# Two samples of the input stored and loaded in blocks of 32 channels: a Fourier filter with a token router, on one core

## The chip, the core and the metric

The kernel runs on one core of a Trainium2 chip. The metric is the device time of one execution in microseconds (us). A run of this kernel varies by about 0.2% around its median, so a difference of less than 0.5% is hard to tell from no change.

## The reference

```python
X = np.fft.rfft(x, axis=1)                  # x: 8 samples, 3136 tokens, 256 channels, float32
Y = X * (filt_r + 1j * filt_i)[None]        # one filter value per frequency and channel
x = np.fft.irfft(Y, n=3136, axis=1)
scores = einsum('bsd,d->bs', x, w_gate)
for b in range(8):
    top = the 128 tokens of sample b with the highest scores
    ye = relu(x[b, top] @ w1) @ w2          # 256 -> 1024 -> 256
    out[b, top] += sigmoid(scores[b, top])[:, None] * ye
```

## The kernel before

**The transform.** 3136 tokens are 98 times 32. The transform of a sample is done in two levels. The *outer* level is a transform of length 98, done for a block of 32 channels at a time, so a sample has 8 blocks ("chunks", c = 0 to 7). The *inner* level is a transform of length 32 with the twiddle factors in its matrices, done for two frequency rows at a time (`i`, 13 of them, taken in pairs: i0 = 0, 2, ... 12; the text writes "step i0"). The work of a stage t is the inner level of sample t and, beside it, the outer level backwards of sample t-1 and forwards of sample t+1.

**A forward chunk** (`outer`) reads its 32 channels from the tile `X`, which holds one sample (4 MB): half 0 holds channels 0 to 127 (chunks 0 to 3), half 1 the others (chunks 4 to 7). Each chunk needs the sum and the difference of two parts of X ("folds", L449). The table `FOLD` says for each sample and chunk, by two letters for sum and difference, who makes them: `p` is GpSimd (POOL), `x` leaves the fold to TensorE, which then multiplies both parts and adds in PSUM, at two more matmuls for the pair. Then come the matmuls (`amm`, L475; 4 of them for `pp`, 6 with one `x`, 8 for `xx`) into a PSUM buffer (`pa`, `pz` or `pv`; there is one buffer of each; `ARING` says which), and a transpose by VectorE (DVE) from there into the tile `UU` (`tout`, L479). A fold into a tile of its own takes one of 3 buffers `s`.

**An inner step** is matmuls into `pz` (`zmm`, L378), two copies to `q` by ScalarE (ACT, L396), two products by DVE with the table `fa` (`pmul`, L400), two by POOL with the table `fb` (`qmul`, L403), matmuls into `pv` (`vmm`, L387), two copies from there by ACT (`vout`, L412) and four score sums by DVE (`gate`, L418). `pz` and `pv` have one buffer each: the next `zmm` waits until DVE has read `pz`, the next `vmm` until the four score sums have read `pv`.

**A backward chunk** is a DVE transpose (L440), matmuls and copies into `X`, from where a half is stored (L595) and the next sample's half is loaded (L600). The table `BACK` says by which form: for `e` one copy is made by ACT and a sum and a difference by DVE (L520); for `p` ACT makes two copies and POOL the sum and the difference (L536). The first ends with DVE as the last reader of the PSUM buffer, the second with ACT.

**The router and the two-layer network.** A search by thresholds (`select`) finds the 128 best tokens of a sample. `SELM` says for each sample whether its comparisons run on DVE (1) or ACT (0). The network on the chosen tokens runs at the end, after the last inner step.

**Order.** `op(...)` only appends a closure to a list; the time and cost arguments in it do nothing at run time. The table `ORDER`, a list of closure numbers, sets the order of the program on every engine. All direct transfers are issued by SyncE (SP), in that order. They share 8 completion semaphores in turn: transfer n+8 is issued only after transfer n has landed, and SP does nothing else while it waits.

**Start.** TensorE first runs 60 small matmuls on zeros (`WARM`, L1064), and later `FILL` groups of them between other work. SP issues half 1 of sample 0, the outer-level matrix (`wa`, 96 KB), half 0, then tables: `fa` and `fb` for steps 4 and 6 (1 MB each), `tf`, `wg`, `ti`, `fb` and `fa` for step 0 (512 KB each). Then comes sample 1 by halves, between the remaining tables. `raw` is a transfer of 8 KB that DVE casts (L1055) between two inner steps.

```python
X = const.tile([128, 2, N2, D // 2], F32, name="X")
def load(when, b, h, bias=0.0):
    def f():
        if b < B:
            nc.sync.dma_start(out=X[:, h].rearrange("p n d -> p (n d)"), in_=x[b, :, h, :N2 * HD])
    op(when, "sp", 5.2, f, ["boot"], [("x", h, c) for c in range(h * n, h * n + n)], lat=2, bias=bias)
```

## Time and profile before

| | |
|---|---|
| median of 3 runs | 465.06 us (464.37 to 466.39) |
| profiled execution | 467.14 us |
| its span in the trace | 465.4 us, so 1.74 us lie around it |
| TensorE busy / DVE / POOL / ACT | 438.7 / 373.4 / 296.7 / 258.2 us |
| granted TensorE clock, mean | 0.997 of full speed |
| moved by DMA | 77.43 MB, 166 GB/s over the span |

A busy TensorE is not one at its peak: small matmuls on zeros count as busy, and matmuls overlap. Idle time of an engine costs something only where others wait for it, so the chain of waits and the timeline of a stretch say more than the shares.

### The profile page before, as it was taken

What the parts mean: (1) busy time and instruction counts of PE and PEld (TensorE: products, weight loads), DVE (VectorE), ACT (ScalarE), POOL (GpSimd) and SP (SyncE); (2) the same over time, 40 slices, a digit from 0 to 9 for tenths busy, and PEclk for the clock granted to TensorE, in tenths of its full rate; (3) what the DMA queues carried; (4) which work ended last, traced back from release to release, by engine and by line L of the source; (5) the groups of instructions that cost most, each with busy time, mean ns of one, the idle gap of its engine ahead of it and who ended that gap; (6) DMA issues with size and microseconds to landing.
All of it is one profiled execution on the core that took longest, in us unless ns stands there. A gap on an engine that the chain in (4) does not pass through costs nothing.

```text
span 465.4 us, 10712 instructions
## 1 busy us (share of the span) xinstructions
PE 438.7 (94%) x4066; PEld 233.8 (50%) x4066; DVE 373.4 (80%) x1079; ACT 258.2 (55%) x611; POOL 296.7 (64%) x262
## 2 busy tenths in 40 slices
...
GB/s 339 372 417 423 208 180 40 2 183 149 265 94 287 32 165 193 140 182 161 208 101 220 135 224 83 238 119 239 87 53 7 156 155 192 176 37 148 164 24 56
DMA packets 61063, 77.43 MB, mean 166 GB/s; under 512 B 3284, under 2 KB 56788, under 8 KB 58324
## 3 DMA queue, kind: packets, MB, share of 16 engines
...
q0 software_dynamic: 768, 2.10, 1.5%
...
HBM read 49.80 MB, written 26.94 MB: 165 GB/s over the span
## 4 chain that ended last, share of the span: by engine, by line
PE 53%; DVE 17%; POOL 9%; issue 6%; DMA 6%; ACT 3%; POOLq 0%; DVEq 0%; SPq 0%; ACTq 0%
PE pv L387 13%; PE py L573 10%; PE pa L475 9%; PE pz L378 7%; DVE rj L418 6%; DMA X<-in_x_dram 4%; DVE t L440 4%; POOL q L403 3%; DVE UU L479 3%; POOL s L449 3%; POOL X L449 2%; DVE y L400 2%; PE pv L953 2%; PE pa L983 2%; DMA out_dram<-X 2%
## 5 line engine op out<-in xcount | busy, mean ns | idle before, releaser
L403 POOL TENSOR_TENSOR q<-q,fb_sb 128x512 f32<-128x512 f32 (+1 forms) x104 | 130.9, 1276 | 67.5 <-ACT q L396 60.9
L449 POOL TENSOR_TENSOR s<-X 113x512 f32<-113x512 f32 x60 | 76.0, 1273 | 55.8 <-DMA X<-in_x_dram 51.2
L573 PE MATMUL py<-t,c_sb 128*98 128x512 f32 x186 | 100.8, 624 | 3.2 <-ACT X L576 2.4
L418 DVE SCALAR_TENSOR_TENSOR rj<-pv,wg_sb 128x256 bf16<-128x256 f32 x199 | 83.6, 420 | 13.9 <-ACT UU L412 7.3
L479 DVE STREAM_TRANSPOSE UU<-pa 128x1024 f32<-128x1024 f32 x59 | 73.3, 1243 | 23.8 <-PE pa L475 23.5
L396 ACT COPY q<-pz 128x512 f32<-128x512 f32 (+1 forms) x104 | 56.3, 586 | 51.5 <-PE pz L378 49.6
L412 ACT COPY UU<-pv 128x512 f32<-128x512 f32 x96 | 51.7, 589 | 56.2 <-PE pv L387 56.0
L440 DVE STREAM_TRANSPOSE t<-UU 128x1024 f32<-128x1024 f32 x64 | 78.8, 1232 | 3.1 <-PE py L573 1.2
L475 PE MATMUL pa<-X,c_sb 49*64 49x512 f32 x344 | 79.8, 601 | 0.4 <-DVE rj L418 0.3
L400 DVE TENSOR_TENSOR y<-pz,fa_sb 128x512 f32<-128x512 f32 (+1 forms) x104 | 67.9, 674 | 8.5 <-ACT q L396 8.5
L387 PE MATMUL pv<-y,ti_sb 64*64 64x256 f32 x796 | 68.7, 386 | 4.2 <-DVE rj L418 3.1
L576 ACT COPY X<-py 98x512 f32<-98x512 f32 x93 | 54.2, 583 | 28.2 <-PE py L573 13.3
L387 PE MATMUL pv<-q,ti_sb 64*64 64x256 f32 x796 | 66.6, 377 | 2.8 <-POOL q L403 2.8
L378 PE MATMUL pz<-UU,tf_sb 64*64 64x256 f32 x800 | 60.9, 395 | 5.4 <-DVE y L400 2.8
L475 PE MATMUL pa<-s,c_sb 49*64 49x512 f32 x220 | 59.1, 606 | 1.3 <-DVE UU L479 1.2
L449 POOL TENSOR_TENSOR X<-X 113x512 f32<-113x512 f32 x42 | 53.2, 1271 | 1.6
L378 PEld LDWEIGHTS pz<-UU,tf_sb 64*64 64x64 f32 x800 | 29.0, 131 | 39.8 <-issue 11.7
L387 PEld LDWEIGHTS pv<-y,ti_sb 64*64 64x64 f32 x796 | 29.9, 132 | 33.5 <-issue 9.5
L573 PEld LDWEIGHTS py<-t,c_sb 128*98 128x98 f32 x186 | 23.9, 163 | 38.0 <-issue 11.5
L387 PEld LDWEIGHTS pv<-q,ti_sb 64*64 64x64 f32 x796 | 34.6, 133 | 15.1 <-POOL q L403 4.2
L679 ACT ACTIVATE junk<-R,nb 128x392 bf16<-128x392 f32 x48 | 30.0, 625 | 12.0 <-DVE nb L698 11.1
L475 PEld LDWEIGHTS pa<-X,c_sb 49*64 49x64 f32 x344 | 20.1, 132 | 15.3 <-issue 10.6
...
## 6 DMA issues: line engine op xcount, KB each, us to landing
...
```

Source lines behind the costliest of these rows:

```text
L378: nc.tensor.matmul(half(z, k)[o, hi], lhsT=tf_sb[p, l], rhs=urow(b, l, 0, D)[p], start=True, stop=True)
L387: nc.tensor.matmul(half(v, k)[o, j], lhsT=ti_at[p, t, i, hi], rhs=y[p, hi], start=t == 0, stop=t == 1)
L396: nc.scalar.copy(out=q[:np_], in_=half(h["z"], k)[:np_])
L400: nc.vector.tensor_tensor(out=y[:np_], in0=half(h["z"], k)[:np_], in1=fa_sb[:np_, i], op=ALU.mult)
L403: nc.gpsimd.tensor_tensor(out=h["q", k][:np_], in0=h["q", k][:np_], in1=fb_sb[:np_, i], op=ALU.mult)
L418: nc.vector.scalar_tensor_tensor(out=rj, in0=half(h["v"], k)[:, j], scalar=1.0, in1=wg_sb, op0=ALU.mult, op1=ALU.mult, accum_out=urow(b, l ...
L440: nc.vector.transpose(out=h["t"].rearrange("p d (l j) -> p d l j", j=2), in_=uchan(b_out, c))
L449: (nc.gpsimd if fold[k] == "p" else nc.vector).tensor_tensor(out=out, in0=two[0], in1=two[1], op=(ALU.add, ALU.subtract)[k])
L475: nc.tensor.matmul(a[o, w].rearrange("p (n d) -> p n d", d=CW), lhsT=lhs[p], rhs=rhs[p], start=n == 0, stop=n == len(terms) - 1)
L479: nc.vector.transpose(out=uchan(b_in, c), in_=h["a"].rearrange("p w (n d) -> p d n w", d=CW))
L573: nc.tensor.matmul(yp[:N1], lhsT=cc["wi"][:, :N1], rhs=h["t"][:, n * CY:(n + 1) * CY].rearrange("p a b -> p (a b)"), start=True, stop=True)
L576: nc.scalar.copy(out=X[:N1, hx, :, at], in_=e["y"][:N1])
```

## The change

1. In DRAM (`kernel`, on the host) and in SBUF (`Xc`), samples 0 and 1 lie by chunk: the 32 channels of a chunk are 4 KB in one row per partition. Samples 2 to 7 lie by halves as before.
2. Each of these two samples comes in 8 transfers of 512 KB, one per chunk, in place of 2 of 2 MB. Folds and matmuls of the two samples read the chunk's own piece.
3. A new ORDER, and with it other letters in `FOLD`, `BACK`, `SELM`, the tables of PSUM buffers (`BRING`, `YRING`, `VRING`, `ARING`) and 8 groups of filling matmuls (47) in place of 12 (57).

```diff
-        "pp pp xp xx pp xp xp xp",
-        "xp px xx pp xp xx pp pp",
-        "xp pp px pp xp xx pp px",
-        "pp pp pp pp px px xp xp",
+        "pp pp xx xx pp xp xp xp",
+        "xp px xp xx pp xx pp pp",
+        "xp pp pp pp xp xx pp pp",
+        "pp pp pp pp px pp xp xp",
...
-    BACK=["ffffffff", "ffffffff", "ffffffff", "ffffffff", "ffffffff", "ffffffff", "peqegggg", "ppppffff"],
+    BACK=["ffffffff", "ffffffff", "ffffffff", "ffffffff", "ffffffff", "ffffffff", "ppqegggg", "ppppffff"],
...
-    SELM=[0, 1, 1, 0, 0, 1, 1, 1],
+    SELM=[0, 0, 1, 0, 0, 1, 1, 1],
...
-    FILL=[6, 8, 12, 5, 5, 2, 2, 2, 3, 4, 2, 6],
+    FILL=[7, 12, 5, 5, 2, 3, 7, 6],
...
+    Xc = X.rearrange("p t n d -> p (t n d)").rearrange("p (c h n d) -> p c h n d", c=D // CW, h=2, d=CW)
...
-            two = Xh[:RW2, hx, 0, :, at], Xh[:RW2, hx, 1, :, at]
+            xin = [Xc[:, c, k] if b_in < 2 else Xh[:, hx, k, :, at] for k in range(2)]
+            two = [xin[k][:RW2] if b_out < 0 else Xh[:RW2, hx, k, :, at] for k in range(2)]
...
+        def piece(c):
+            nc.sync.dma_start(out=Xc[:, c].rearrange("p h n d -> p (h n d)"), in_=x[b, :, h, c % n * N2 * CW:(c % n + 1) * N2 * CW])
+
         n = HD // CW
+        if b < 2:
+            for c in range(h * n, h * n + n):
+                op(when + .01 * (c % n), "sp", 5.2 / n, lambda c=c: piece(c), ["boot"], [("x", h, c)], lat=2, bias=bias)
+            return
...
-    data["x"][..., :-XPAD] = xs.reshape(B, 128, N2, 2, D // 2).transpose(0, 1, 3, 2, 4).reshape(B, 128, 2, -1)
+    for b in range(B):
+        n = 2 if b >= 2 else 8
+        data["x"][b, ..., :-XPAD] = xs[b].reshape(128, N2, n, D // n).transpose(0, 2, 1, 3).reshape(128, 2, -1)
```

**The transfers at the start, on SP.** Before, from the first transfer to the first half of sample 1 (rows of 4096 floats are halves, 2048 and 1024 in `fa` and `fb` are 1 MB and 512 KB):

```order
L600 DMA X<-in_x_dram 128x4096
L1076 DMA c_sb<-in_cst_dram 128x192
L600 DMA X<-in_x_dram 128x4096
L1043 DMA fa_sb<-in_fri_dram 128x2048
L1043 DMA fb_sb<-in_fri_dram 128x2048
L1079 DMA tf_sb<-in_tf_dram 128x1600
L1080 DMA wg_sb<-in_moe_w_gate_dram 128x256
L1102 DMA ti_sb<-in_ti_dram 128x3328
L1043 DMA fb_sb<-in_fri_dram 128x1024 [waits DMAHW0_49]
L1043 DMA fa_sb<-in_fri_dram 128x1024 [waits DMAHW1_49]
L600 DMA X<-in_x_dram 128x4096 [waits DMAHW2_49,PE_49,Pool_49]
```

Now, to the same place (the pieces of sample 0 are those of chunks 5, 4, 6, then 0, 3, 2, 7, then 1; the first of sample 1 is chunk 1's):

```order
L605 DMA X<-in_x_dram 128x1024 x3
L1086 DMA c_sb<-in_cst_dram 128x192
L605 DMA X<-in_x_dram 128x1024 x4
L605 DMA X<-in_x_dram 128x1024 [waits DMAHW0_49]
L1053 DMA fa_sb<-in_fri_dram 128x2048 [waits DMAHW1_49]
L1053 DMA fb_sb<-in_fri_dram 128x2048 [waits DMAHW2_49]
L1089 DMA tf_sb<-in_tf_dram 128x1600 [waits DMAHW3_49]
L1112 DMA ti_sb<-in_ti_dram 128x3328 [waits DMAHW4_49]
L1090 DMA wg_sb<-in_moe_w_gate_dram 128x256 [waits DMAHW5_49]
L605 DMA X<-in_x_dram 128x1024 [waits DMAHW0_49,DMAHW6_49,PE_49,Pool_49]
L1053 DMA fa_sb<-in_fri_dram 128x1024 [waits DMAHW7_49]
L1053 DMA fb_sb<-in_fri_dram 128x1024
```

The tables for step 0 (the two rows of 1024 in `fa` and `fb`) moved from ahead of sample 1 to behind its first piece, and that piece waits for TensorE and POOL to be done with chunk 1 of sample 0. Behind these rows the other pieces of sample 1 come in the order 0, 3, 2, 4, 5, 6, 7, with `raw` and the two tables for step 2 between those of chunks 3 and 2, and the two tables of 1.25 MB for steps 8 to 12 between 4 and 5.

**POOL, from the end of the start into the first inner steps.** Before, from chunk 7's fold of sample 0 on:

```order
L449 TENSOR_TENSOR s<-X 113x512 [waits DMAHW2_49,PE_49]
L449 TENSOR_TENSOR X<-X 113x16x32 [waits Pool_49]
L449 TENSOR_TENSOR s<-X 113x512 [waits PE_49] x2
L449 TENSOR_TENSOR X<-X 113x16x32 [waits Pool_49]
L403 TENSOR_TENSOR q<-q,fb_sb 128x512 [waits DMAHW4_49,Activation_49]
L403 TENSOR_TENSOR q<-q,fb_sb 128x512 [waits Activation_49]
L403 TENSOR_TENSOR q<-q,fb_sb 128x512 [waits DMAHW0_49,Activation_49]
L403 TENSOR_TENSOR q<-q,fb_sb 128x512
L449 TENSOR_TENSOR s<-X 113x512 [waits DMAHW2_49,PE_49,Pool_49]
L403 TENSOR_TENSOR q<-q,fb_sb 128x512 [waits DMAHW5_49,PE_49,Activation_49]
```

Now, from chunk 7's fold on:

```order
L451 TENSOR_TENSOR s<-X 113x512 [waits DMAHW7_49,PE_49]
L451 TENSOR_TENSOR s<-X 113x512 [waits DMAHW4_49,PE_49]
L451 TENSOR_TENSOR X<-X 113x512 [waits Pool_49]
L451 TENSOR_TENSOR s<-X 113x512 [waits DMAHW0_49,PE_49]
L451 TENSOR_TENSOR X<-X 113x512 [waits Pool_49]
L404 TENSOR_TENSOR q<-q,fb_sb 128x512 [waits DMAHW2_49,Activation_49]
L404 TENSOR_TENSOR q<-q,fb_sb 128x512 [waits Activation_49]
L404 TENSOR_TENSOR q<-q,fb_sb 128x512 [waits DMAHW0_49,Activation_49]
L451 TENSOR_TENSOR s<-X 113x512 [waits DMAHW6_49,PE_49,Pool_49]
L404 TENSOR_TENSOR q<-q,fb_sb 128x512 [waits Activation_49]
L451 TENSOR_TENSOR s<-X 113x512 [waits DMAHW1_49,PE_49]
L404 TENSOR_TENSOR q<-q,fb_sb 128x512 [waits DMAHW4_49,PE_49,Activation_49]
```

One fold of sample 0 is gone (chunk 2's), and the first fold of sample 1 (chunk 1's) moved from behind the two products of step 0 to between them; the next two folds, of chunks 0 and 2, stand one product apart.

**DVE, in the backward chunks 1 and 3 of sample 6.** Before, from a backward transpose to the next four score sums (the two rows of L520 are the sum and the difference of chunk 1; those of chunk 3 follow behind the score sums):

```order
L440 STREAM_TRANSPOSE t<-UU 128x1024
L696 TENSOR_SCALAR ok,J<-pm 128x15
L698 TENSOR_SCALAR nb<-J,nd 128x1
L520 TENSOR_TENSOR X<-pa,X 113x16x32
L400 TENSOR_TENSOR y<-pz,fa_sb 128x512
L520 TENSOR_TENSOR X<-pa,X 113x16x32
L400 TENSOR_TENSOR y<-pz,fa_sb 128x512
L418 SCALAR_TENSOR_TENSOR rj,UU<-pv,wg_sb 128x256 x4
```

Now:

```order
L441 STREAM_TRANSPOSE t<-UU 128x1024
L401 TENSOR_TENSOR y<-pz,fa_sb 128x512
L706 TENSOR_SCALAR ok,J<-pm 128x15
L708 TENSOR_SCALAR nb<-J,nd 128x1
L401 TENSOR_TENSOR y<-pz,fa_sb 128x512
L419 SCALAR_TENSOR_TENSOR rj,UU<-pv,wg_sb 128x256 x4
```

Chunk 1's two operations have left DVE; the score sums come two operations earlier.

## Rows read from the trace of the kernel before

**Rows 1.** The page: TensorE's busy time; GB/s moved in 40 equal slices (11.635 us each).
```profile
PE 438.7 (94%) x4066; PEld 233.8 (50%) x4066; DVE 373.4 (80%) x1079; ACT 258.2 (55%) x611; POOL 296.7 (64%) x262
...
GB/s 339 372 417 423 208 180 40 2 183 149 265 94 287 32 165 193 140 182 161 208 101 220 135 224 83 238 119 239 87 53 7 156 155 192 176 37 148 164 24 56
```
**Rows 2.** Stretches: busy time of each engine (instructions), granted clock, DMA share, GB/s.
```profile
0.00:25.00 25.00, 22.95 (x240) 15.32 (x244) 9.46 (x8) 1.49 (x2) 12.84 (x16) 1.00 0.91 360
25.00:67.00 42.00, 38.35 (x498) 23.85 (x494) 29.57 (x73) 14.20 (x27) 32.43 (x26) 1.00 0.74 297
67.00:112.00 45.00, 45.00 (x412) 20.08 (x407) 40.07 (x94) 30.53 (x80) 25.04 (x20) 1.00 0.34 118
...
337.00:382.00 45.00, 38.83 (x406) 18.72 (x404) 42.56 (x139) 27.90 (x62) 23.07 (x19) 1.00 0.39 96
```
**Rows 3.** Timeline 0 to 25 us: start, duration, engine, line, [idle before, what ended it].
```profile
8.37 0.33 SPq L1043 DMA_DIRECT2D fb_sb<-in_fri_dram  x1
8.43 3.70 POOL L449 TENSOR_TENSOR s<-X 113x512 f32<-113x512 f32 x3 [7.50 <-DMA X<-in_x_dram]
...
9.92 0.65 PE L475 MATMUL pa<-X,c_sb 49*64 49x512 f32 x2
...
16.18 1.27 POOL L449 TENSOR_TENSOR X<-X 113x512 f32<-113x512 f32 x1
...
18.85 1.25 DVE L479 STREAM_TRANSPOSE UU<-pa 128x1024 f32<-128x1024 f32 x1 [1.82 <-PE pa L475]
...
19.98 1.28 POOL L449 TENSOR_TENSOR X<-X 113x512 f32<-113x512 f32 x1
...
24.73 1.14 PE L378 MATMUL pz<-UU,tf_sb 64*64 64x256 f32 x16 [0.55 <-DVE UU L479]
```
**Rows 4.** DMA packets started in 0 to 6 us, and in 26 to 28 us.
```profile
DMA packets 96, 1.57 MB, mean 262 GB/s; under 512 B 0, under 2 KB 0, under 8 KB 0
...
DMA packets 200, 0.88 MB, mean 441 GB/s; under 512 B 29, under 2 KB 29, under 8 KB 185
```
**Rows 5.** Timeline 30 to 61 us: TensorE's second matmuls of a step, POOL's folds of sample 1.
```profile
30.82 2.52 POOL L403 TENSOR_TENSOR q<-q,fb_sb 128x512 f32<-128x512 f32 x2 [1.73 <-ACT q L396]
...
34.49 0.66 PE L387 MATMUL pv<-y,ti_sb 64*64 64x256 f32 x8 [0.41 <-DVE rj L418]
...
35.04 1.26 POOL L449 TENSOR_TENSOR s<-X 113x512 f32<-113x512 f32 x1 [1.70 <-DMA X<-in_x_dram]
...
41.48 0.66 PE L387 MATMUL pv<-y,ti_sb 64*64 64x256 f32 x8
...
48.33 0.66 PE L387 MATMUL pv<-y,ti_sb 64*64 64x256 f32 x8 [0.26 <-DVE rj L418]
...
48.84 1.27 POOL L449 TENSOR_TENSOR s<-X 113x512 f32<-113x512 f32 x1 [0.24 <-DMA X<-in_x_dram]
...
60.29 0.66 PE L387 MATMUL pv<-y,ti_sb 64*64 64x256 f32 x8 [0.26 <-DVE rj L418]
```
**Rows 6.** Groups by form: POOL on rows in one piece (q) and on blocks of 32 (folds).
```profile
L403 POOL TENSOR_TENSOR q<-q,fb_sb 128x512 f32<-128x512 f32 x96 | 120.7, 1276 | 59.5 <-ACT q L396 52.9 <-PE pa L475 4.4 <-ACT UU L412 1.3
...
L449 POOL TENSOR_TENSOR s<-X 113x512 f32<-113x512 f32 x60 | 76.0, 1273 | 55.8 <-DMA X<-in_x_dram 51.2 <-PE pa L475 4.3
```
**Rows 7.** Timeline 354 to 366 us: the backward chunks 1 and 3 of sample 6.
```profile
354.49 2.52 POOL L403 TENSOR_TENSOR q<-q,fb_sb 128x512 f32<-128x512 f32 x2 [9.67 <-ACT q L396]
...
361.15 0.69 DVE L520 TENSOR_TENSOR X<-pa,X 113x512 f32<-113x512 f32 x1
...
362.35 0.68 DVE L520 TENSOR_TENSOR X<-pa,X 113x512 f32<-113x512 f32 x1
...
363.18 1.13 PE L505 MATMUL pa<-t,c_sb 64*64 64x512 f32 x8 [1.37 <-DVE X L520]
...
365.52 0.66 PE L387 MATMUL pv<-y,ti_sb 64*64 64x256 f32 x8 [0.30 <-DVE rj L418]
```
**Rows 8.** Waits, longest in total first: who waited for whom, us, times, longest.
```profile
POOL s L449 <- DMA X<-in_x_dram: 51.2, 11, 8.8
```

24 lines of the change are left out of this document (12 added, 12 removed), and 192 rows, old and new, of tables (FOLD, ORDER).

## The prediction

> **What bounds the kernel now.** I read the page first. TensorE is busy for 438.7 of 465.4 us [rows 1], so there is little idle time to win, and the question is where it lies. The stretches answer that [rows 2]: in 67 to 112 us TensorE is busy all the time. It idles for 2.0 us in the first 25 us, 3.7 us in 25 to 67 (zeros count as busy there, so the true wait is larger), and 6.2 us in 337 to 382. The granted clock is full in all of them. The change acts on the first two stretches and, by new letters, on the last.
>
> The start: the timeline [rows 3] shows POOL idle for 7.50 us until the first half of x has landed; SP saw it land at 8.37. TensorE comes to its first real matmul at 9.92, behind its 60 matmuls on zeros. POOL then makes ten folds from 8.43 to 21.26 (19.98 and 1.28), almost without a gap. Chunk 0's difference ends at 17.45 (16.18 and 1.27), and 1.40 us later, at 18.85, DVE begins the first of five transposes that follow each other without a gap; it had waited 1.82 us for TensorE. The first inner step starts behind them, at 24.73. So the start is a chain: landing, POOL's folds, DVE's transposes.
>
> The first inner steps: the matmuls into `pv` start at 34.49 (step 0), 41.48 (step 2), 48.33 and, two steps on, 60.29 [rows 5], mostly released by DVE's score sums: a loop through one PSUM buffer. POOL waited 1.70 us for the first half of sample 1, until 35.04, and 0.24 us for the second, until 48.84. From 11.6 to 46.5 us the transfers ran at 372 to 423 GB/s [rows 1], so all these bytes stand in one full queue, and their place in it says when they land.
>
> **The change, step by step.** *First landing.* By 6.0 us 1.57 MB had moved [rows 4]. That is three pieces of 0.524 MB. The first half (2.10 MB) would be moved by 7.3 at the 0.417 MB per us of the third slice [rows 1] and was seen at 8.37: a landing lag of 1.1 us. The third piece, chunk 6's, which POOL folds first, then lands at 7.1, and POOL starts 1.3 us earlier. Chunk 7's piece (3.77 MB with the matrix) lands at about 12.4, when POOL has done four folds (12.2).
>
> *POOL and DVE.* One fold of 1.27 us is gone (nine, not ten); chunk 2 costs TensorE two matmuls more, which lie beside the folds. Chunk 0's difference is POOL's seventh fold in both orders: 7.1 + 7 x 1.27 + 0.2 = 16.2 instead of 17.45. With 1.40 us to DVE and the same five transposes, the first inner step starts at 24.73 - 1.2 = 23.5. DVE now takes chunk 4 before chunk 6, which idles it for a microsecond ahead of 17.6, but not after. The smaller fold count therefore wins nothing beyond the earlier landing: chunk 1's folds end near 18.7, before TensorE wants them. Chunks in one piece don't make a fold faster: products on rows in one piece take 1276 ns, folds on blocks of 32 take 1273 [rows 6]. TensorE can't start earlier either; its zeros still end at 9.9.
>
> *Tables and sample 1.* By the slices 3.94, 8.27 and 13.1 MB have moved at 11.6, 23.3 and 34.9 us [rows 1]. In the old order the first half of sample 1 ends at 12.19 MB, which is 23.3 + 3.92 / 0.417 = 32.7 us, and the fold began at 35.04 after a wait for it: a lag of 2.3 us here. In the new order `fb` for step 0 ends at 10.61 MB (it stood at 9.57): moved by 28.9, landed by 30.0 with the lag of the start and by 31.2 with the later one. POOL wants it at 30.82 - 1.2 = 29.6. So it is 0.4 to 1.6 us late. Between the two products now stands chunk 1's fold, whose piece (9.57 MB) has landed by 28.7. Three operations of 1.27 us end at 33.8 or 35.0, and the matmuls of step 0 start then, not at 34.49 - 1.2 = 33.3. The new place of the fold pays back one operation later: chunk 1's DVE transpose (1.25 us) stood between steps 0 and 2 and now runs while DVE would wait for those matmuls. The interval of 6.99 us (34.49 to 41.48) falls to 5.7, and step 2 starts at 39.5 or 40.8: 2.0 or 0.7 us earlier than before. Chunk 2's fold, which stands in front of step 2's second product, needs a piece at 13.24 MB (35.2, landed 37.5), is done with the product at 40.0, and holds nothing up. I take the middle, **1.3 us**, because the lag was measured at both values. It contains the 1.2 us of the start.
>
> *Does it stay?* Behind step 2 the order on DVE is the old one, so the loop keeps its intervals. The pieces of chunks 5, 6 and 7 end at 16.9, 17.4 and 18.3 MB, so the last is moved at 47.1 and landed at 49.4, as late as the second half before (48.84). But that half held four chunks, and now only chunk 7 waits for the end; 11 us lie between that landing and the step at 60.29. The queue itself ends no sooner: no byte is saved, and the 14 additional issues stand on an SP that waits most of the time. From 67 us on TensorE is full [rows 2], so what is won before 67 stays won.
>
> *Sample 6, backward chunk 1.* TensorE waited 1.37 us at 363.18 for DVE's sum and difference (0.69 and 0.68 us), and the next matmuls into `pv`, at 365.52, again waited for DVE [rows 7]. With `p` those two operations move to POOL, which idled 9.67 us at 354.49, and one copy more to ACT. The gain lies between 0 (another wait takes the place) and 1.4; I take **0.9**, as both waits named DVE.
>
> *The rest.* Nine folds of sample 1 stay nine. One fold in all samples goes from TensorE to POOL, eight comparisons of sample 1's search from DVE to ACT, and 10 filling matmuls go: 0, since they lie beside a full TensorE or in idle time. The reordering of samples 2 to 7 swaps neighbours; its price isn't in any row. The bounds are a gain of the 6.2 us that TensorE idles in 337 to 382 and a loss of 8.8 us, POOL's longest wait for a half of x [rows 8]. I take 0, nearest to the stretch 67 to 112 where no idle time is left to move, and keep 1.5 us to either side for it.
>
> Sum: 1.3 + 0.9 = 2.2 us, or 467.14 - 2.2 = 464.9 for an execution like the profiled one. That one lay 2.1 us above the median of the runs, 465.06, which gives **462.9**.
>
> **A rule that speaks against it.** Transfers of 4 KB rows ran beside each other without loss: in 26 to 28 us, 156 of 200 packets were of 2 to 8 KB, and 441 GB/s moved [rows 4]. The Trainium skill (DMA: Bandwidth & Descriptors, "Rules for kernel authors") asks for at least 1 MiB per transfer for full bandwidth, and by its fixed cost of about 2.0 us a piece of 0.524 MB would take some 3.2 us; paid one after the other, eight pieces would end 12 us later than my sum has it. The row disagrees: the fixed part overlaps with the next transfer.
>
> **The rivals.** *More comes of it* (0.24): the lag is 1.1 throughout, sample 6 gives its whole 1.4 us, and the search and the sums that leave DVE (sample 1's eight comparisons) or the new order free another microsecond: 2.0 + 1.4 + 0.8 = 4.2, so 460.9. For it: the waits in rows 7. Against it: the lag of 2.3 at 35 us.
>
> *Nothing much comes of it* (0.20): `fb` for step 0 lands at 31.2 or later, step 2 gains 0.7, the last chunk is late by as much, and at 363 another wait takes over: 0 to 0.7 us, so 464.7. For it: the table moved back in a queue that was already full.
>
> *Slower* (0.12): halves of samples 2 to 7. POOL waits for them 11 times, 51.2 us in all [rows 8]; a half is loaded only when its chunks are read and the last sample's half is stored. If the new order puts one operation of 1.27 us in front of the last chunk of a half, the load is issued later by that and TensorE follows, once per stage: six stages, 7.6 us. It decides when more than three of the six stages lose it: 4.5 - 2.2 is 0.5%. With four to five, 468. Against it: the same tables and form of the stages.
>
> *The pieces don't come one by one* (0.05): the 16 DMA engines serve all queued pieces in turn, so that no piece is in before the last, near 13.6. POOL starts 5.2 us later than at 8.43, and the whole start slips: 470. By the Trainium skill's fixed cost one after the other it would be some 12 us, 477. Against both: the first half landed by 8.37 with 2 MB queued behind it [rows 3].
>
> **The numbers.** The forecast (0.39) stands for 461.7 to 464.3. A difference within 0.5% (462.7 to 467.4) is about what a measurement can't tell from no change. A little under half of the forecast and all of the first rival lie below it: faster 0.42. The rest of the forecast, the second rival and a little of the third lie within: 0.43. Slower: 0.15. The range, 460.0 to 466.8, leaves out the far end of the first rival and most of the last two.
>
> **What would show it.** Right: POOL's first fold near 7.1, the first inner step near 23.5, step 0's product in POOL held by `fb` until 30 or 31, step 2's matmuls at 39.5 to 40.8, no wait of TensorE for L522 at 361. Wrong: a first fold after 8.4; a first inner step after 24.7; step 2 after 41.5; a stage after 67 us longer than its old one by over a microsecond, with POOL waiting for x; or a granted clock below full in the first 25 us, where fewer zeros are now multiplied.

## The result and the profile after

The changed kernel took 460.19 us (median of 4 runs, 458.54 to 461.35), the kernel before 464.78 us in 4 runs beside it: a ratio of 0.9892 [0.9853, 0.9932], or 4.6 us less. The forecast was 2.2 us less. The profiled execution took 461.35 us with a span of 459.6.

The page after: TensorE is as busy as before [rows 1], 438.3 us; POOL's products take 1275 ns and its folds, on rows in one piece now, 1273 [rows 6].

```profile
PE 438.3 (95%) x4042; PEld 234.0 (51%) x4042; DVE 368.9 (80%) x1053; ACT 263.5 (57%) x636; POOL 300.4 (65%) x265
...
L404 POOL TENSOR_TENSOR q<-q,fb_sb 128x512 f32<-128x512 f32 (+1 forms) x104 | 131.1, 1275 | 60.0 <-ACT q L397 58.4
L451 POOL TENSOR_TENSOR s<-X 113x512 f32<-113x512 f32 x59 | 74.6, 1273 | 54.2 <-DMA X<-in_x_dram 47.4
```

The same stretches as in rows 2, after (TensorE is busy for 0.6 us more in the second and 1.0 us more in the last), and the wait of rows 8:

```profile
0.00:25.00 25.00, 22.92 (x230) 15.00 (x234) 9.33 (x8) 1.49 (x2) 11.65 (x15) 1.00 0.93 367
25.00:67.00 42.00, 38.96 (x503) 24.44 (x495) 31.09 (x76) 14.84 (x28) 33.70 (x27) 1.00 0.80 311
67.00:112.00 45.00, 44.31 (x414) 19.61 (x413) 39.64 (x94) 31.63 (x85) 28.39 (x23) 1.00 0.31 101
337.00:382.00 45.00, 39.81 (x419) 19.66 (x417) 42.35 (x138) 29.23 (x64) 24.76 (x20) 1.00 0.38 95
...
POOL s L451 <- DMA X<-in_x_dram: 47.4, 10, 9.2
```

The timeline of the start after, against rows 3:

```profile
7.45 2.49 POOL L451 TENSOR_TENSOR s<-X 113x512 f32<-113x512 f32 x2 [6.51 <-DMA X<-in_x_dram]
...
13.86 2.50 POOL L451 TENSOR_TENSOR s<-X 113x512 f32<-113x512 f32 x2 [1.36 <-DMA X<-in_x_dram]
...
18.88 1.25 DVE L481 STREAM_TRANSPOSE UU<-pa 128x1024 f32<-128x1024 f32 x1 [2.61 <-PE pa L477]
...
24.75 1.14 PE L379 MATMUL pz<-UU,tf_sb 64*64 64x256 f32 x16 [0.67 <-DVE UU L481]
```

POOL begins 1 us earlier than at 8.43, waits 1.36 us for chunk 7's piece, and the first inner step starts at 24.75, where it was 24.73. **The start gave nothing.**

The timeline of the first inner steps after, against rows 5:

```profile
30.36 1.28 POOL L404 TENSOR_TENSOR q<-q,fb_sb 128x512 f32<-128x512 f32 x1 [1.24 <-ACT q L397]
...
34.51 0.80 PE L388 MATMUL pv<-y,ti_sb 64*64 64x256 f32 x6
...
35.28 1.24 DVE L481 STREAM_TRANSPOSE UU<-pa 128x1024 f32<-128x1024 f32 x1
...
39.97 0.43 PE L388 MATMUL pv<-y,ti_sb 64*64 64x256 f32 x2
...
47.32 0.66 PE L388 MATMUL pv<-y,ti_sb 64*64 64x256 f32 x8
...
49.33 1.29 POOL L451 TENSOR_TENSOR s<-X 113x512 f32<-113x512 f32 x1 [0.50 <-DMA X<-in_x_dram]
...
52.42 0.66 PE L388 MATMUL pv<-y,ti_sb 64*64 64x256 f32 x8
...
58.44 0.66 PE L388 MATMUL pv<-y,ti_sb 64*64 64x256 f32 x8 [0.52 <-DVE rj L419]
...
63.14 0.44 PE L379 MATMUL pz<-UU,tf_sb 64*64 64x256 f32 x1
```

The corresponding rows of before that stand nowhere above, its step 8 and the first inner matmul of stage 1:

```profile
53.44 0.66 PE L387 MATMUL pv<-y,ti_sb 64*64 64x256 f32 x8
...
64.98 0.44 PE L378 MATMUL pz<-UU,tf_sb 64*64 64x256 f32 x1
```

(The steps run in the order 4, 0, 2, 6, 8, 10, 12.) From step 0 on the intervals were 6.99, 6.85, 5.11 and 6.85 us [rows 5] and are now 5.46, 7.35, 5.10 and 6.02. Two became shorter, by 1.53 and 0.83; one became 0.50 longer. So the first stage ends 1.84 us earlier in these two profiles. The kernel before, B2, E7, E8 and E10 (all below) run the same program up to this point and end the stage at 64.81 to 65.34 us; the changed kernel, E6, H1 and H2 run the same new one and end it at 63.14 to 63.91. By these means the gain is about 1.6 us, and a single profile can't tell differences of half a microsecond in the end of this stage.

The longer interval is the one from step 2 to 6 (6.85, now 7.35; 6.84 to 7.23 in E6, H1 and H2). By the timeline it may be chunk 3's letter `xx`: 16 matmuls of that chunk stand ahead of step 6's, where 8 stood before. No run tested it. The two intervals from step 0 to 6 together are 12.81 to 13.14 us in the four traces of the new program and 13.84 to 14.23 in the five of the old, so they give about 1.0 us.

```profile
45.50 1.97 PE L477 MATMUL pa<-X,c_sb 49*64 49x512 f32 x16
```

The timeline of the last inner stage after, against rows 7; its first inner matmul is at 348.84, before it was at 352.62:

```profile
348.84 1.14 PE L379 MATMUL pz<-UU,tf_sb 64*64 64x256 f32 x16 [0.32 <-DVE UU L481]
...
355.44 0.64 PE L388 MATMUL pv<-y,ti_sb 64*64 64x256 f32 x8
...
360.54 0.66 PE L388 MATMUL pv<-y,ti_sb 64*64 64x256 f32 x8 [0.35 <-DVE rj L419]
...
370.84 0.61 PE L388 MATMUL pa<-y,ti_sb 64*64 64x256 f32 x8
...
375.24 0.63 PE L388 MATMUL pv<-y,ti_sb 64*64 64x256 f32 x8
```

And the same in before:

```profile
352.62 1.14 PE L378 MATMUL pz<-UU,tf_sb 64*64 64x256 f32 x16 [0.32 <-DVE UU L479]
...
359.56 0.66 PE L387 MATMUL pv<-y,ti_sb 64*64 64x256 f32 x8
...
375.85 0.66 PE L387 MATMUL pv<-y,ti_sb 64*64 64x256 f32 x8
...
381.11 0.66 PE L387 MATMUL pv<-y,ti_sb 64*64 64x256 f32 x8 [0.77 <-ACT q L396]
```

(Here the steps run in the order 8, 0, 6, 2, 4, 10, 12.) Counted from the stage's start, the first group of second matmuls came at 6.94 us and now comes at 6.60; the second (365.52 in rows 7) at 12.90 and now 11.70; the fourth at 23.23 and now 22.00; the fifth at 28.49 and now 26.40. Of the 1.2 us at the second group, 0.86 lies between the first and the second (5.96, now 5.10): that is the letter `p`. The other 0.34 lies ahead of the first group and comes with the new order of the stage; it is not kept to the end (E8, below, doesn't have it and has the same tail). Another 0.86 lies between the fourth and the fifth (5.26, now 4.40), where the fourth group, step 2's, goes to `pa` and not to `pv`: a letter of `VRING` that stands in the change's tables and that the prediction did not cost.

The spans of the two profiles (465.37 and 459.57 us) differ by three parts. I call **first stage** all up to the first inner matmul of stage 1 (64.98, now 63.14: 1.84 less), **middle** from there to the first one of stage 7 (287.63, now 285.70: 1.93 less) and **tail** the rest (112.75, now 110.73: 2.02 less). Two traces can't tell chance from cause; the experiments give the same three numbers for every run.

### The profile page after: what moved, and what is told of

Read it like the earlier page. It is cut to its first block, busy times and chain, and to the rows that moved or that the text cites. A ratio compares the mean times of both kernels' runs of the same rounds, so it can differ in the third digit from the quotient of the medians.

```text
span 459.6 us, 10703 instructions
## 1 busy us (share of the span) xinstructions
PE 438.3 (95%) x4042; PEld 234.0 (51%) x4042; DVE 368.9 (80%) x1053; ACT 263.5 (57%) x636; POOL 300.4 (65%) x265
## 3 DMA queue, kind: packets, MB, share of 16 engines
q1 hardware_dynamic: 61972, 74.65, 49.1%
## 4 chain that ended last, share of the span: by engine, by line
PE 62%; DVE 11%; issue 6%; POOL 6%; DMA 6%; ACT 3%; POOLq 0%; DVEq 0%; ACTq 0%; SPq 0%
PE pv L388 16%; PE py L575 12%; PE pa L477 10%; PE pz L379 8%; DVE rj L419 4%; DMA X<-in_x_dram 3%; POOL s L451 2%; DMA out_dram<-X 2%; DVE t L441 2%; DVE y L401 2%; PE pv L963 2%; PE pa L993 2%; PE pm L575 2%; POOL X L451 2%; POOL q L404 1%
## 5 line engine op out<-in xcount | busy, mean ns | idle before, releaser
L404 POOL TENSOR_TENSOR q<-q,fb_sb 128x512 f32<-128x512 f32 (+1 forms) x104 | 131.1, 1275 | 60.0 <-ACT q L397 58.4
L451 POOL TENSOR_TENSOR s<-X 113x512 f32<-113x512 f32 x59 | 74.6, 1273 | 54.2 <-DMA X<-in_x_dram 47.4
L575 PE MATMUL py<-t,c_sb 128*98 128x512 f32 x182 | 98.7, 624 | 2.7 <-ACT X L578 1.9
L419 DVE SCALAR_TENSOR_TENSOR rj<-pv,wg_sb 128x256 bf16<-128x256 f32 x195 | 81.8, 420 | 13.1 <-ACT UU L413 7.2
L481 DVE STREAM_TRANSPOSE UU<-pa 128x1024 f32<-128x1024 f32 x58 | 72.0, 1241 | 10.8 <-PE pa L477 10.3
L477 PE MATMUL pa<-X,c_sb 49*64 49x512 f32 x332 | 76.9, 602 | 1.4 <-POOL X L451 0.8
L388 PE MATMUL pv<-y,ti_sb 64*64 64x256 f32 x780 | 67.4, 386 | 3.5 <-DVE rj L419 2.7
L578 ACT COPY X<-py 98x512 f32<-98x512 f32 x91 | 53.0, 583 | 29.3 <-PE py L575 15.9
L388 PE MATMUL pv<-q,ti_sb 64*64 64x256 f32 x780 | 65.4, 376 | 0.0
L477 PE MATMUL pa<-s,c_sb 49*64 49x512 f32 x216 | 57.6, 605 | 1.2 <-POOL s L451 0.7
L451 POOL TENSOR_TENSOR X<-X 113x512 f32<-113x512 f32 x44 | 55.8, 1273 | 1.2
L379 PEld LDWEIGHTS pz<-UU,tf_sb 64*64 64x64 f32 x800 | 28.9, 131 | 39.5 <-issue 14.8
```

The costliest lines, as they stand in the source:

```text
L379: nc.tensor.matmul(half(z, k)[o, hi], lhsT=tf_sb[p, l], rhs=urow(b, l, 0, D)[p], start=True, stop=True)
L388: nc.tensor.matmul(half(v, k)[o, j], lhsT=ti_at[p, t, i, hi], rhs=y[p, hi], start=t == 0, stop=t == 1)
L404: nc.gpsimd.tensor_tensor(out=h["q", k][:np_], in0=h["q", k][:np_], in1=fb_sb[:np_, i], op=ALU.mult)
L419: nc.vector.scalar_tensor_tensor(out=rj, in0=half(h["v"], k)[:, j], scalar=1.0, in1=wg_sb, op0=ALU.mult, op1=ALU.mult, accum_out=urow(b, l ...
L451: (nc.gpsimd if fold[k] == "p" else nc.vector).tensor_tensor(out=out, in0=two[0], in1=two[1], op=(ALU.add, ALU.subtract)[k])
L477: nc.tensor.matmul(a[o, w].rearrange("p (n d) -> p n d", d=CW), lhsT=lhs[p], rhs=rhs[p], start=n == 0, stop=n == len(terms) - 1)
```

## The experiments

All runs together. All times are us. "First" is the first inner matmul; a star marks a trace whose granted clock fell near 378 us, in the tail.

| run | us | before beside it | ratio [95%] | first | first stage | middle | tail |
|---|---|---|---|---|---|---|---|
| before | | | | 24.73 | 64.98 | 287.63 | 112.75 |
| after | 460.19 | 464.78 | 0.9892 [0.9853, 0.9932] | 24.75 | 63.14 | 285.70 | 110.73 |
| E1 | 464.92 | 464.78 | 1.0004 [0.9987, 1.0022] | 24.50 | 68.20 | 284.82 | 110.72 |
| E2 | 464.67 | 464.78 | 1.0005 [0.9989, 1.0020] | 24.70 | 65.14 | 285.32 | 112.70 |
| E3 | 459.96 | 464.78 | 0.9896 [0.9872, 0.9921] | 24.32 | 62.70 | 284.48 | 110.93 |
| E4 | 460.09 | 464.78 | 0.9890 [0.9864, 0.9915] | 24.47 | 63.62 | 285.57 | 110.74 |
| E5 | 465.15 | 464.01 | 1.0031 [1.0006, 1.0057] | 24.47 | 65.83 | 285.75 | 113.98* |
| E6 | 462.72 | 464.01 | 0.9960 [0.9940, 0.9980] | 24.83 | 63.21 | 285.22 | 112.69 |
| E7 | 463.48 | 464.01 | 0.9982 [0.9964, 1.0000] | 24.66 | 64.97 | 284.31 | 113.08* |
| E8 | 462.63 | 464.01 | 0.9960 [0.9940, 0.9981] | 24.57 | 64.81 | 287.03 | 110.75 |
| E9 | 464.97 | 464.42 | 1.0015 [0.9995, 1.0036] | 24.09 | 65.21 | 285.46 | 113.95* |
| E10 | 462.79 | 464.42 | 0.9965 [0.9948, 0.9982] | 24.71 | 65.34 | 285.82 | 111.62 |
| E11 | 462.75 | 464.42 | 0.9958 [0.9942, 0.9974] | 24.68 | 65.45 | 285.17 | 110.73 |
| E12 | 459.60 | 464.42 | 0.9893 [0.9870, 0.9916] | 23.62 | 63.02 | 287.81 | 110.72 |
| E13 | 461.11 | 464.79 | 0.9907 [0.9884, 0.9930] | 23.35 | 63.81 | 285.88 | 110.75 |
| H1 | 462.97 | 464.09 | 0.9978 [0.9956, 1.0000] | 24.78 | 63.91 | 285.56 | 113.98* |
| H2 | 460.83 | 464.09 | 0.9931 [0.9913, 0.9949] | 25.02 | 63.69 | 286.18 | 110.74 |
| H3 | 460.48 | 464.09 | 0.9918 [0.9896, 0.9939] | 24.54 | 63.76 | 284.88 | 110.72 |
| H4 | 462.03 | 464.09 | 0.9953 [0.9931, 0.9975] | 24.58 | 63.98 | 285.55 | 110.73 |
| B2 | 463.94 | 464.79 | 1.0004 [0.9976, 1.0031] | 24.55 | 65.14 | 283.88 | 112.35 |

### Pieces or order?

**E1, the new order with halves:** each half of samples 0 and 1 comes in one transfer, at the place of its first piece.

```diff
+            if b in (0, 1):
+                if c == {(0, 1): 5, (0, 0): 0, (1, 0): 1, (1, 1): 4}[b, h]:
+                    nc.sync.dma_start(out=Xc[:, h * n:h * n + n].rearrange("p c h n d -> p (c h n d)"), in_=x[b, :, h, :N2 * HD])
+                return
```

> The changed kernel, but samples 0 and 1 come in halves of 2 MB again (chunk layout kept), each half issued at the place of its first piece. Theory A: the pieces carry the gain, because the new order puts 2 MB of sample 1 in front of the tables of step 0; the products of step 0 on POOL then wait for fb some 3.5 us longer (1.5 MB more in front at 0.42 MB/us), POOL starts at 8.4 and not 7.4, and the time goes to 463.5 to 466. Theory B: the gain is the order and the letters alone: the time stays at 460 to 461, the first zmm of sample 1 stays near 63.1.

**E2, the old order with pieces:** the kernel before, samples 0 and 1 by chunk, the four pieces of a half issued where the half was.

```diff
-            if b < B:
+            if b < 2:
+                for c in {(0, 1): (6, 5, 4, 7), (0, 0): (0, 2, 3, 1), (1, 0): (1, 2, 0, 3), (1, 1): (5, 4, 7, 6)}[b, h]:
+                    nc.sync.dma_start(out=Xc[:, c].rearrange("p h n d -> p (h n d)"), in_=x[b, :, h, c % n * N2 * CW:(c % n + 1) * N2 * CW])
+            elif b < B:
```

> The kernel before (its order and all its letters) with the layout by chunk and 8 pieces for samples 0 and 1, each half's 4 pieces issued where the half was. Theory A (pieces carry the gain): POOL starts its folds near 7.3 and not 8.4, sample 1's first zmm comes 1 to 1.8 us before 64.98, the time falls to 463.0 to 463.8. Theory B (order and letters carry it): first zmm of sample 0 and of sample 1 as before (24.7, 65.0), the time stays at 464.5 to 465.2.

**E3, as E1 for sample 0 alone** (`if b in (0,):`).

> The changed kernel with sample 0 alone in halves of 2 MB; sample 1 in pieces. My theory after the first comparison: the start gave no gain (first zmm 24.75 against 24.73), since POOL took its 1 us lead into a wait for chunk 7's piece. So this is the same as the changed kernel within 0.3 us: 460.0 to 460.6, first zmm 24.7 to 25.3. Rival: the earlier start of the folds does pay by freeing DVE for later; then it loses 1 us, 461.2 or more.

Measured: E1 and E2 are both no change, and E3 is as fast as the changed kernel. As built here, neither the order nor the pieces gain anything alone; together they are worth 1%. The pieces of sample 0 are worth nothing (E3). Why E1 gains nothing, in its timeline and its stretches:

```profile
33.70 1.28 POOL L404 TENSOR_TENSOR q<-q,fb_sb 128x512 f32<-128x512 f32 x1 [4.83 <-DMA fb_sb<-in_fri_dram]
...
25.00:35.00 10.00, 6.94 (x110) 5.22 (x102) 3.78 (x10) 3.22 (x6) 3.79 (x4) 0.96 1.01 415
35.00:45.00 10.00, 9.36 (x88) 4.45 (x82) 5.14 (x13) 3.00 (x6) 7.52 (x7) 0.70 1.01 423
```

A half of 2.10 MB now stands ahead of the tables for step 0. POOL waits 4.83 us for `fb`, TensorE is busy for 6.94 of 10 us, and in the next 10 us its granted clock is 0.70 of the full 2.4 GHz. The first stage ends at 68.20 and takes back what the tail gains. So E1 prices halves at this place of the queue. Halves of sample 1 placed behind the tables of step 0 weren't run with the new order. Why E2 gains nothing, in its timeline:

```profile
4.76 3.79 POOL L451 TENSOR_TENSOR s<-X 113x512 f32<-113x512 f32 x3 [3.83 <-DMA X<-in_x_dram]
...
12.06 1.28 POOL L451 TENSOR_TENSOR s<-X 113x512 f32<-113x512 f32 x1 [2.16 <-PE pa L477]
...
18.82 1.25 DVE L481 STREAM_TRANSPOSE UU<-pa 128x1024 f32<-128x1024 f32 x1 [1.82 <-PE pa L477]
...
38.23 1.28 POOL L404 TENSOR_TENSOR q<-q,fb_sb 128x512 f32<-128x512 f32 x1 [3.69 <-PE pa L477]
```

POOL begins 3.7 us earlier than before and then waits for TensorE to give back a buffer `s`; the transpose at 18.82 is where it was. At 38.23 the profile puts POOL's next wait, 3.69 us, down to TensorE; but `fb` of step 2, which now stands behind four pieces, landed only at 38.07, and in the kernel before, at 37.41. So the wait is most likely one for this table, as in E5 below.

### Can the start be made worth something?

**E4:** in the changed kernel the folds and matmuls of one chunk of the start are moved one chunk ahead on POOL and TensorE.

```diff
-    2, 0, 1, 17, 16, 18, 11, 12, 15, 53, 14, 46, 19, 47, 13, 50, 54, 29, 48, 56, 51, 49, 34, 30, 55, 57, 35, 52, 38,
+    2, 0, 1, 17, 16, 18, 11, 12, 15, 53, 14, 46, 19, 47, 13, 50, 54, 29, 48, 34, 51, 49, 35, 56, 30, 55, 36, 52, 57,
```

> The changed kernel with the folds and matmuls of chunk 0 put ahead of chunk 7's at the start (chunk 0's piece landed at 8.9, chunk 7's at 13.9). If the start's chain is what held the first inner step, POOL no longer idles 1.36 us, chunk 0's difference ends near 14.5 instead of 17.7, and the first zmm comes at 22.5 to 23.5 instead of 24.75; the time then falls by 0.8 to 2.2 us against the changed kernel, 458.0 to 459.4. Rival: tables for the first steps land when they land, the products of step 0 wait for fb (30.4), and all of the gain is used up there: 460 to 460.5, the matmuls into pv at 34.5 as before.

**E12, as E4, and DVE takes its first two transposes in the other order.**

```diff
-    2, 0, 1, 17, 16, 18, 11, 12, 15, 53, 14, 46, 19, 47, 13, 50, 54, 29, 48, 34, 51, 49, 35, 56, 30, 55, 36, 52, 57,
+    2, 0, 1, 17, 16, 18, 11, 12, 15, 53, 14, 46, 19, 47, 13, 50, 54, 29, 48, 34, 51, 55, 49, 35, 56, 30, 36, 52, 57,
```

> The changed kernel with chunk 0 ahead of chunk 7 at the start, as in the earlier run (which gained nothing: TensorE waited 0.9 us at 15.7 for the buffer that chunk 6's transpose frees), and now DVE takes chunk 6 before chunk 4. If the chain of the start then is TensorE's matmuls alone, the first transpose is at 12.0 in place of 13.2, the first zmm at 23.4 to 23.9 in place of 24.5. Theory A (what the start wins stays won): the time falls 0.5 to 1.0 us below the changed kernel, to a ratio of 0.987 to 0.988. Theory B (the first products wait for their tables, as fb of step 0 lands near 30): ratio 0.989 to 0.990 as the changed kernel, the second zmm group not earlier than 28.2.

**E13, as E12, and `fa` and `fb` for step 0 are issued ahead of sample 1's first piece.**

```diff
-    38, 20, 37, 42, 39, 33, 58, 44, 43, 40, 45, 41, 21, 60, 3, 91, 93, 25, 98, 95, 99, 26, 100, 94, 59, 4, 67, 92, 62,
+    38, 20, 37, 42, 39, 33, 58, 44, 43, 40, 45, 41, 21, 25, 26, 60, 3, 91, 93, 98, 95, 99, 100, 94, 59, 4, 67, 92, 62,
```

> The run in which DVE takes chunk 6 first (first zmm at 23.6, but POOL then waited 2.6 us for fb of step 0), with the two tables of step 0 issued ahead of sample 1's first piece. Theory A (that wait is all that took the start's lead away): POOL's first product of step 0 at 29.4 to 29.8 and not 30.6, step 0's matmuls into pv at 33.0 to 33.5 and not 34.1, sample 1's first zmm at 62.0 to 62.5, the time 0.6 to 1.2 us below the changed kernel, a ratio of 0.9865 to 0.9885. Theory B (the next transfers in the full queue, piece 1 and the tables of step 2, are then late instead): as the changed kernel, 0.989 to 0.991.

Measured: the first inner step moved from 24.75 to 24.47, 23.62 and 23.35, and the end of the first stage from 63.14 to 63.62, 63.02 and 63.81. None is faster than the changed kernel beyond the intervals. E12's timeline shows who takes the time, and the second fence is E13's:

```profile
23.62 1.14 PE L379 MATMUL pz<-UU,tf_sb 64*64 64x256 f32 x16 [0.66 <-DVE UU L481]
...
30.59 1.28 POOL L404 TENSOR_TENSOR q<-q,fb_sb 128x512 f32<-128x512 f32 x1 [2.60 <-DMA fb_sb<-in_fri_dram]
```

```profile
30.67 1.28 POOL L404 TENSOR_TENSOR q<-q,fb_sb 128x512 f32<-128x512 f32 x1 [2.95 <-DMA fb_sb<-in_fri_dram]
...
38.31 1.28 POOL L451 TENSOR_TENSOR s<-X 113x512 f32<-113x512 f32 x1 [1.16 <-DMA X<-in_x_dram]
```

A start that is 1.1 us earlier only waits longer for `fb`, which lands at 30.5. With the tables ahead of the piece, `fb` lands no sooner and the third fold of sample 1 now waits for its piece. The wait moved from one customer of the full queue to another. The trace marks the landing of each transfer in 16 shares: the first share of `fb` came 1.45 us sooner in E13 (27.23, in E12 28.68), the last did not (30.53 and 30.46). Why the last one didn't stays open.

### What in the first stage?

**H4, the changed kernel with its first three folds of sample 1 one place later** (chunk 1's behind both products of step 0, as before, and its matmuls behind step 0's).

```diff
-    69, 74, 71, 23, 70, 28, 96, 149, 75, 101, 27, 5, 79, 97, 76, 150, 102, 81, 61, 146, 86, 24, 68, 63, 151, 88, 87,
-    32, 72, 82, 152, 77, 6, 103, 78, 83, 153, 105, 73, 31, 110, 107, 80, 154, 157, 111, 147, 106, 84, 158, 64, 89,
+    69, 74, 71, 23, 70, 28, 96, 75, 101, 27, 5, 79, 97, 76, 149, 102, 81, 61, 146, 86, 24, 68, 63, 88, 150, 87, 32,
+    72, 82, 151, 152, 77, 6, 103, 78, 83, 153, 105, 73, 31, 110, 107, 80, 154, 157, 111, 147, 106, 84, 158, 64, 89,
```

> The changed kernel with chunk 1 of sample 1 where it stood: its fold behind both products of step 0, its matmuls behind step 0's second matmuls, its transpose behind the products of step 2. Theory A (the forecast's mechanism: the transpose stood between steps 0 and 2): the interval from step 0's to step 2's matmuls into pv goes from 5.5 to 6.7 to 7.0 us, with step 0's up to 1.2 earlier, so step 2's are 0.3 to 1.5 us later, and the time is 0.3 to 1.5 above the changed kernel. Theory B: step 0's matmuls come as much earlier as the interval grows, no change.

**H3, the changed kernel with chunk 4 of sample 1 as before** (TensorE makes its sum).

```diff
-        "xp px xp xx pp xx pp pp",
+        "xp px xp xx xp xx pp pp",
```

> The changed kernel with chunk 4 of sample 1 in xp and not pp: POOL makes its difference alone, TensorE multiplies both parts for the sum, as before. Theory A (TensorE's two more pairs of matmuls stand in the loop ahead of step 10): the interval from step 8's to step 10's matmuls into pv goes from 6.0 to 6.4 to 6.9 us, sample 1's first zmm comes 0.4 to 0.8 later, the time is 0.4 to 0.8 above the changed kernel. Theory B (hidden): no change.

Measured, H4's timeline first, then H3's:

```profile
34.34 0.66 PE L388 MATMUL pv<-y,ti_sb 64*64 64x256 f32 x8 [1.14 <-DVE rj L419]
...
38.07 1.25 DVE L481 STREAM_TRANSPOSE UU<-pa 128x1024 f32<-128x1024 f32 x1 [1.48 <-PE pa L477]
...
41.20 0.75 PE L388 MATMUL pv<-y,ti_sb 64*64 64x256 f32 x8
```

```profile
52.21 0.66 PE L388 MATMUL pv<-y,ti_sb 64*64 64x256 f32 x8
...
59.06 0.66 PE L388 MATMUL pv<-y,ti_sb 64*64 64x256 f32 x8 [0.52 <-DVE rj L419]
```

In H4 the interval from step 0 to 2 is 6.86 us again, where the changed kernel has 5.46: chunk 1's transpose is back at 38.07, ahead of step 0's score sums; in the changed kernel it ran at 35.28. In H4 DVE idles for 1.48 us just ahead of it, and step 0's score sums begin at 39.24, in the changed kernel at 37.98. The four traces of the changed kernel's first stage (after, E6, H1, H2) have 5.46 to 6.27 for this interval, the five of the old program 6.98 to 7.37. From step 0 to 6 H4 has 13.83, as the old program. In H3 the interval from step 8 to 10 is 6.85 again and not 6.02: it is 6.02 or 6.03 in every trace in which POOL makes chunk 4's sum, and 6.85 or 6.86 in every trace in which TensorE does. The ends of the two first stages, 63.98 and 63.76, lie about where the same new program ends it anyway (63.14 to 63.91), so the intervals are the evidence here, not the ends. By time, beside the same runs of the kernel before, H4 gains 2.1 us, H3 3.6 and H2 (below) 3.3.

In the changed kernel chunk 4 has a piece of its own, and POOL folds it at 40.98 and 42.33, while in the kernel before it came with a half that landed at 48.84 [rows 5]. That chunk 4's gain needs pieces is not shown: E1, with halves, has 6.02 too. The shorter interval from step 0 to 2 is in neither: E1 has 7.37 for it and E2 7.14.

**E5 and E9 copy these moves into the old order with pieces (E2).** E5 puts the fold of chunk 1 between step 0's products; E9 also orders the tables and pieces on SP as the changed kernel does up to step 2.

```diff
-    25, 68, 94, 64, 6, 72, 26, 95, 90, 142, 74, 30, 79, 22, 7, 61, 80, 75, 81, 143, 65, 29, 70, 139, 96, 144, 76, 98,
+    25, 68, 94, 142, 64, 6, 72, 26, 95, 143, 90, 74, 30, 79, 22, 7, 61, 144, 80, 75, 81, 65, 29, 70, 139, 96, 76, 98,
```

> The kernel before in pieces (the second experiment of the first group: no gain) and one move: chunk 1's fold of sample 1 goes between the two products of step 0 on POOL, its matmuls ahead of step 0's second matmuls, its transpose ahead of step 2's products on DVE. Theory A (this move is what the pieces pay for): the interval from step 0's to step 2's matmuls into pv falls from 7.0 us to about 5.5, as in the changed kernel, sample 1's first zmm comes at 63.2 to 64.0 in place of 65.1, the time falls by 1.1 to 1.9 us, to 462.8 to 463.6. Theory B (the gain needs the tables of step 0 behind the first piece, or the other letters of sample 1): step 2's matmuls gain less than 0.5, the time stays at 464.3 to 465.0.

> The kernel before in pieces, with chunk 1's fold between the products of step 0 (as in the run that lost 0.3%), and now also the order of transfers of the changed kernel: piece 1, the tables of step 0, pieces 0 and 3, the small constants and the tables of step 2, pieces 2 and 4, the last tables, pieces 5, 6, 7. Theory A (the pieces pay because tables go in between them): POOL's wait of 3.9 us for step 2's table goes, step 2's matmuls into pv come at 39.7 to 40.3, sample 1's first zmm at 63.0 to 63.8, the time 1.3 to 2.0 us below the kernel before. Theory B (the other letters of sample 1, or more of the new order, are needed): first zmm after 64.3, the time less than 0.7 us below.

Measured: no gain; the first stage ends at 65.83 and 65.21. In E5 POOL waits 3.91 us, until 38.91, for `fb` of step 2, which now stands behind four pieces; in E9 that wait is 0.22 us, but `fb` of step 0 comes at 31.40. The interval from step 0 to 2 is short in both (5.84 and 5.17), but step 0 starts some 2 us later (36.43 and 36.57, before 34.49), which takes it back. The single moves that were tried don't carry over.

**H1, the changed kernel up to stage 1's first inner matmul, and the kernel before from there on, with the old letters; H2, the same with the letters `p` and `pa`.** H1 has the changed kernel's rows of `FOLD` for samples 0 and 1 and its `FILL`; H2 besides:

```diff
-    BACK=["ffffffff", "ffffffff", "ffffffff", "ffffffff", "ffffffff", "ffffffff", "peqegggg", "ppppffff"],
+    BACK=["ffffffff", "ffffffff", "ffffffff", "ffffffff", "ffffffff", "ffffffff", "ppqegggg", "ppppffff"],
-    VRING=["vvvvvva", "vvvvvvv", "vvvvvvv", "vvvvvvv", "vvvvvvv", "vvvvvvv", "vvvvvvv", "vvvvvvv"],
+    VRING=["vvvvvva", "vvvvvvv", "vvvvvvv", "vvvvvvv", "vvvvvvv", "vvvvvvv", "vvvvvvv", "vavvvvv"],
```

> The changed kernel up to the first inner step of sample 1 (pieces, order, letters and fillings of samples 0 and 1), and from there the kernel before: its order, its letters, its search. Theory A (the new first stage is worth 1.9 us by itself, and keeps it): sample 1's first zmm at 62.7 to 63.3, the time 1.6 to 2.2 us below the kernel before. Theory B (stages that follow give it back, the old order was tuned to its own first stage): less than 1.0 us below.

> The kernel of the run before this one, with the two letters at the end: p for chunk 1 of sample 6 and pa for step 2 of sample 7. Theory A (first stage 1.9, end 1.9, the reordering of samples 1 to 6 some 0.8): 3.6 to 4.2 us below the kernel before, 0.4 to 1.0 above the changed kernel. Theory B (the middle gives nothing): as the changed kernel, 4.4 to 4.8 below. Theory C (the middle gives much): 3.2 us or less below.

Measured: H1 is 0.2% faster, at the edge of what can be told from no change, with a first stage that is 1.07 us shorter; H2 is 0.7% faster (3.3 us), which is what its first stage (1.3) and its tail (2.0) give together.

### What in the tail?

**E7: the kernel before with `p`; E8: with `p` and `pa`; E10: with `pa` alone; E11: E9 with both.** The two rows of tables are those above; in E8 and E10 the next step's second matmuls (step 4's) also stand ahead of step 2's last two score sums in `ORDER`, as the second buffer allows.

> The kernel before with one letter: chunk 1 of sample 6 goes back by p and not by e, so its sum and difference move from DVE to POOL, behind chunk 0's. Theory A (these two operations on DVE were 1.2 us on the path): TensorE's wait of 1.37 us ahead of the matmuls of chunk 3 goes, sample 7's stage from first to last zmm falls from 32.55 to 31.2 to 31.4, the time to 463.4 to 463.8. Theory B (a new wait takes the place, POOL's products come later behind the two additional operations): 464.5 to 465.0.

> The kernel before with both letters: p for chunk 1 of sample 6, and pa for the second matmuls of step 2 of sample 7. Theory A (the two letters are the whole 2.0 us of the stage, and they add up): first to last zmm 30.4 to 30.7 in place of 32.55, the time 462.6 to 463.0. Theory B (part of it needs the rest of the new order): first to last zmm above 31.0, the time above 463.3.

> The kernel before with one letter: the second matmuls of step 2 of sample 7 go to pa. Theory A (it adds up with the other letter): the interval to the next such matmuls falls from 5.26 to 4.4 us, sample 7's stage from first to last zmm from 32.55 to 31.7, the time 0.6 to 1.0 us below the kernel before. Theory B (it only pays with p): the same time as before within 0.4 us.

> The kernel before with three edits alone: sample 1 in pieces with the tables between them and chunk 1's fold between the products of step 0; p for chunk 1 of sample 6; pa for step 2 of sample 7. Theory A (these carry nearly all of the gain; the reordering of samples 2 to 6, SELM and the fillings are worth at most 0.6 us): the time is 3.3 to 4.2 us below the kernel before, 0 to 0.9 above the changed kernel. Theory B (the reordering of the middle matters): 2.5 us or less below the kernel before.

**E6: the changed kernel without `pa`** (and with step 4's second matmuls behind both of these score sums again).

```diff
-    VRING=["vvvvvva", "vvvvvvv", "vvvvvvv", "vvvvvvv", "vvvvvvv", "vvvvvvv", "vvvvvvv", "vavvvvv"],
+    VRING=["vvvvvva", "vvvvvvv", "vvvvvvv", "vvvvvvv", "vvvvvvv", "vvvvvvv", "vvvvvvv", "vvvvvvv"],
```

> The changed kernel with the second matmuls of step 2 of sample 7 in pv again and not in pa (one letter of the table of these buffers), and the next step's matmuls behind both score sums. Theory A (this letter is 0.8 us of the 2.0 that sample 7's inner stage gained): the interval between these two groups of matmuls goes from 4.4 to 5.2 or 5.3 us, sample 7's stage from first to last zmm from 30.5 to 31.3 or 31.4, the time to 460.8 to 461.2. Theory B (the gain there has another source, such as POOL's earlier sums): no change, 460.0 to 460.4.

Measured: E8 has the changed kernel's tail (110.75) on the old order and is 0.4% faster; E11 has it too, and adds nothing. `pa` alone gives 0.35% (E10; 0.7 to 1.1 us of tail against the three traces of the old tail without a fall of the clock), `p` alone 0.2% (E7, at the edge of no change). E6 loses about 2 us of tail, more than the 0.86 above. Its timeline says why:

```profile
370.56 0.66 PE L388 MATMUL pv<-y,ti_sb 64*64 64x256 f32 x8
...
373.67 1.24 DVE L441 STREAM_TRANSPOSE t<-UU 128x1024 f32<-128x1024 f32 x1
...
376.83 0.66 PE L388 MATMUL pv<-y,ti_sb 64*64 64x256 f32 x8 [1.79 <-DVE rj L419]
```

Up to 370.56 it has the whole gain of `p` (22.12 us from its stage's start at 348.44; before 23.23). Then TensorE waits 1.79 us for score sums that stand behind a backward transpose on DVE; the interval is 6.27 us, and all of it is given back. With `pa` the next group has another buffer and waits for neither. So in the new order `p` makes time that is kept only with `pa`. In the old order it is otherwise. In E7 the fifth group comes at 27.65 us from the stage's start (376.93 less 349.28), before at 28.49, so `p` alone still has its 0.84 there. Then E7's granted clock falls, and the next interval is 6.69 us, in the kernel before 5.10.

**B2, the kernel before once more**, for the clock of its tail.

> The kernel before, unchanged, for a second trace of it. Theory A (its clock falls in part of its executions): either a fall to half near 378 us and 112.8 to 114.0 us from sample 7's first zmm to the end, or a full clock and 112.7; the stretch from sample 1's first zmm to sample 7's between 284 and 287 us, not the 287.6 of the first trace. Theory B (the first trace is typical): full clock and 287.5 again.

Measured: no fall in its trace, a tail of 112.35 and a ratio of 1.0004.

## Why the prediction was right and wrong

*The direction* was right, and the time lies inside the range, just above its lower end of 460.0; the forecast size, 2.2 us, was a little under half of the 4.6 that came. The step that failed in the sum is *"The rest, 0"*: it put every other new letter at nothing without a row for the letter `pa`, and that letter alone gives 0.35% (E10), 0.86 us in the profile and, in the new order, about 2 us of tail (E6). The rival *More comes of it* (460.9) came nearest in time, for other reasons in part: it gave sample 6's form 1.4 us and 0.8 to the search and the order, and had no term for `pa`.

*The start (1.2 us inside the first term)* was wrong. Its failed step is that chunk 7's piece "lands at about 12.4, when POOL has done four folds": POOL had it at 13.86, and as POOL takes chunk 7 before chunk 0, chunk 0 waited with it, though its piece was the fourth and had landed at 8.91. In the trace 14 of the 16 shares of chunk 7's piece had landed by 12.39, the last at 13.72. The last shares fall behind from a 16 KB packet of the instruction queue on, which took 1.07 us at 10.72; that fits in time, but no run removed it, so the cause stays open. The text's own sign of being wrong, "a first inner step after 24.7", came true (24.75). And an earlier start was worth nothing anyhow, because it ends in a wait for `fb` (E12, E13). The text's own estimate, `fb` landed between 30.0 and 31.2, was right (30.14 in the changed kernel). Since the start did not come earlier, `fb` was no wait in the changed kernel: POOL started at 30.36, released by ACT.

*The interval from step 0 to 2* was right in its mechanism (chunk 1's transpose moves into DVE's waiting time) and in its size: forecast 5.7, measured 5.46, and 5.86 to 6.27 in three more traces; H4 shows it. Step 2 came at 39.97, inside the 39.5 to 40.8 (40.44 to 41.04 in E6, H1 and H2). That this time was right rests on two errors that cancel: no gain in the start, and no loss at `fb`.

*"Behind step 2 the order on DVE is the old one, so the loop keeps its intervals"* was wrong twice: the next interval grew (by 0.50 in the profile, by nothing to 0.4 in E6, H1 and H2), and the one from step 8 to 10 fell by 0.83, because chunk 4's sum went to POOL (H3). The prediction counted the folds of sample 1 and did not ask which interval each moved fold stands in. First stage: forecast 1.3, measured 1.84 in the two profiles and about 1.6 over nine. One reading is wrong without harm to the sum: 16 pieces in place of 4 halves are 12 additional issues, not 14.

*Sample 6, `p` (0.9)* was right: 0.86, and TensorE's wait for L522 at 361 is gone, as it said. It did not see that in the new order the next wait on `pv` would take this back without `pa`. *"The rest, 0"* hid that letter. The row that bore on it, the last interval of 5.26 us, was not read, since only stretches with a change of form were looked at, not every changed letter in a stage with idle time.

*The middle, 0*, was right on the average, and partly by luck, as gains and losses cancel in it. The 1.93 us between the first two profiles is chance: over 11 traces with the old order of the middle the mean is 285.6 (283.88 to 287.63), over 9 with the new one 285.5 (284.48 to 287.81). Inside it stage 2 became shorter by about 1.4 us, and stage 3 longer by about 1.6 (48.4 to 49.1 in the new order, before 47.1). So one sign of being wrong, a stage after 67 us longer by over a microsecond, came true, though not with its cause, POOL waiting for x: in that stage POOL waits for x for 2.1 us, before 6.7, and TensorE is busy for 48.1 of 49.1 us, before 45.2 of 47.1. The rival of halves that come late is out: POOL's waits for them fell from 51.2 to 47.4 us. So is the rival of pieces that don't come one by one: E2's POOL folds the first at 4.76 us. The rule of 1 MiB per transfer (the Trainium skill, DMA: Bandwidth & Descriptors, "Rules for kernel authors") would have spoken against the change; here the stretch 25 to 67 us moved 311 GB/s with the pieces and 297 without [rows 2].

*Sum:* about 1.6 for the first stage, 1.9 for the tail (110.73 against a mean of 112.60 in the three traces of the old tail without a fall of the clock) and 0.1 are 3.6 of the 4.6 us, inside the interval (3.2 to 6.8 us by the ratio). Some 0.3 us more may be the clock of the tail, which fell in the old order only (below). The rest, under a microsecond, stays open. It isn't seen in the new order of the middle: H2, with the old middle, and H3, with the new one, ran beside the same runs of the kernel before, have equal first stages (63.69 and 63.76) and tails (110.74 and 110.72), and took 460.83 and 460.48 us, with intervals that overlap. H2's interval overlaps the changed kernel's too. No version beat the changed kernel beyond the intervals.
